# Top-k attention and a tanh-shrink feed-forward on one core: probabilities turned by TensorE in 40 of 144 steps, weight words staged in six places, 128-token feed-forward units, and a look-ahead rate for dealing them

## The chip, the cores and the metric

The program runs on one core of one Trainium2 chip. The metric is the device time of one execution in microseconds (us). The time before is 1709.63 us, the median of three runs (1709.08 to 1714.47).

## What is computed

```python
scores = scale * np.matmul(q, k.transpose(0, 1, 3, 2))     # 8 x 8 heads, 576 x 576, head size 64
kth = np.partition(scores, -top_k, axis=-1)[..., -top_k:-top_k + 1]    # top_k = 32
scores = np.where(scores >= kth, scores, -1000000000.0)
attn = np.exp(scores - np.max(scores, axis=-1, keepdims=True))
attn = attn / (np.sum(attn, axis=-1, keepdims=True) + 1e-09)
x = np.matmul(attn, v)          # then as 4608 tokens x 512
h = x @ w_in                    # 512 x 2048
out = (h - np.tanh(h)) @ w_out  # 2048 x 512
```

The weights arrive as float64, the rest as float32, and all matmuls run in float32, each as two passes in the trace.

## The kernel before

The attention is cut into 144 **steps** (`plan`). A step is 128 query rows of two heads of one batch entry `b`; the last 64 rows of the 576 are gathered over two head pairs into a remainder step (`rem`). For each b there are 16 plain steps, taken in pairs, and 2 remainder steps. Steps are numbered from 0 here. The first `run` takes all of them; the second, exact one is entered only if a flag asks for it.

A step runs through a software pipeline, written out by hand in the loop at the end of `run`. In iteration n the kernel issues, in this order: `values` of step n-4, `spread` of n-3, `mask` of n-1, `search` of n, `spread_keys` of n-2, then `scores` of n+1 and `expo` of n-1, with feed-forward work dealt in between. `manual_schedule` keeps that order on every engine.

- `scores` (L210): TensorE makes the 128 x 576 scores of two heads in PSUM. There is one such buffer, and it comes free when VectorE has done L241 of the step before. ScalarE copies the scores to SBUF (L218).
- `search` (L240 to L251): VectorE folds the two halves of each row by minimum and maximum, then four rounds of MAX8 and MATCH_REPLACE find the 32nd value. A search begins with L240, so L240 marks the start of a step on VectorE.
- `mask` and `expo` (L267 to L317): ScalarE and GpSimd set what is not kept to a very low number and take exponentials; z is the result.
- `turn_z` (L360): VectorE transposes z in blocks of 32 x 32; `spread_keys` (L374): 16 DMAs on SyncE's queue move the blocks, so that `et` holds the transposed z of a pair of steps. There is one `et`.
- `values` (L393, L401): TensorE multiplies `et` with v, once per pair, and turns the spread reciprocals of the sums; ScalarE copies both (L405), and GpSimd multiplies them into the unit's `xT` (L417, L410).

The feed-forward takes **units** of 256 tokens: 16 for the pairs of query blocks and 2 for the remainders of four batch entries each. A unit is 32 items in a first-in-first-out list `work`: 16 of `ffn_h` (L442, four 128 x 256 matmuls, then tanh, copy and subtraction for two of them) and 2 x 8 of `ffn_o` (L462, two 128 x 512 matmuls; the last of a block copies and stores it). `deal` takes items out at four places of an iteration, at a rate that `run` sets anew each time:

```python
more = min([m + 4 for m in done if m + 4 > n], default=n)
share[0] = len(work) / max(more - n, 1)
```

So what is in the list is spread over the iterations until the next unit is ready. At the end of b = 3 and of b = 7, two units come ready one or two steps apart.

The float64 weights are turned into float32 in 32 pieces of 128 x 512 (`convert`): two DMAs of 0.5 MB load the words and the words shifted by three bytes, VectorE does L139, L143 and, later, L149, ScalarE L140, L141 and L146, GpSimd L152. The words lie in two places of `spare`; both DMAs are issued on ScalarE's queue, and a piece's load waits for L149 of the piece two before. The table `many` gives steps 0 to 8 one piece, step 9 four, steps 10 to 16 three each until 32 are done. From step `EARLY` = 17 on, `spare` serves as a second `zx`.

## Time and profile before

| | |
|---|---|
| profiled execution | 1712.53 us, of which the span is 1710.7 us |
| TensorE busy | 1444.8 us (84%) |
| VectorE busy | 1384.2 us (81%) |
| GpSimd busy | 942.8 us (55%) |
| ScalarE busy | 857.9 us (50%) |
| mean granted TensorE clock | 0.94 of full speed |
| moved by DMA | 157.96 MB, mean 92 GB/s |

Busy shares are means over stages with different limits; a stage is read by what its engines do in it, and by what a waiting engine waits for. TensorE's matmuls are pipelined, so a busy TensorE is judged by the spacing of its matmuls. The rows that follow the change come from views of one profiled execution.

### The profile page before, as it was taken

How to read it: one execution, taken by the hardware profiler on the slowest of the kernel's cores; microseconds unless marked ns; L12 is line 12 of the kernel's file. 1: busy time of each engine (PE TensorE's matmuls, PEld its weight loads, DVE VectorE, ACT ScalarE, POOL GpSimd, SP SyncE). 2: the span in 40 equal slices, each digit the busy share in tenths (PEclk: the TensorE clock that was granted, in tenths of full speed). 3: DMA queues.
4: the chain of work that ended last, by engine and by line, in shares of the span. 5: the costliest groups of instructions: out<-in, count | busy, mean ns of one | idle time of the engine just before them, and what ended most of it. 6: DMA issues, size and time to landing. Idle time of an engine off the chain costs nothing.

```text
span 1710.7 us, 24180 instructions
## 1 busy us (share of the span) xinstructions
PE 1444.8 (84%) x6802; PEld 886.7 (52%) x6802; DVE 1384.2 (81%) x3842; ACT 857.9 (50%) x1509; POOL 942.8 (55%) x1517
## 2 busy tenths in 40 slices
PE   1232444899998999899999999899899999899998
PEld 1111332474746474647476564657465646465664
DVE  5986665999989999999945999999999999962800
ACT  2444544455645574556434564566455655442621
POOL 2444544565746584667534665566556666552720
PEclk9956767999999999999999999999999999999999
DMA  6545454453245324532414324533343334310220
GB/s 156 133 136 172 155 175 137 96 109 85 65 102 108 85 66 101 108 82 67 103 28 91 81 62 92 110 86 73 86 105 89 79 84 104 83 48 25 63 49 15
DMA packets 266510, 157.96 MB, mean 92 GB/s; under 512 B 212608, under 2 KB 220800, under 8 KB 266368
## 3 DMA queue, kind: packets, MB, share of 16 engines
q1 hardware_dynamic: 257152, 122.79, 31.9%
q10 hardware_dynamic: 9216, 33.54, 5.8%
q8 instruction: 57, 0.93, 0.2%
q14 instruction: 85, 0.70, 0.1%
HBM read 61.85 MB, written 9.44 MB: 42 GB/s over the span
## 4 chain that ended last, share of the span: by engine, by line
PE 53%; DVE 15%; SPq 14%; DMA 7%; issue 4%; ACT 4%; POOL 2%; ACTq 1%; DVEq 0%; POOLq 0%
PE hps L442 20%; PE ops L462 19%; SPq L374 12%; PE av L393 7%; PE scps L210 6%; DVE m L248 3%; DVE ab L251 3%; DMA spare<-in_moe_w_out_dram 2%; SPq L172 2%; DMA spare<-in_moe_w_in_dram 2%; DVE zx L360 1%; DMA kin<-in_k_dram 1%; DVE f L149 1%; DVE ab L240 1%; DVE ab L243 1%
## 5 line engine op out<-in xcount | busy, mean ns | idle before, releaser
L442 PE MATMUL hps<-xT,w_in 128*128 128x256 f32 x2048 | 484.2, 392 | 56.2 <-ACT g L455 38.4
L462 PE MATMUL ops<-w_out,g 128*128 128x512 f32 x1152 | 526.2, 606 | 0.0
L248 DVE MAX8 m<-ab 128x8 f32<-128x288 f32 (+1 forms) x1152 | 465.0, 446 | 0.0
L442 PEld LDWEIGHTS hps<-xT,w_in 128*128 128x128 f32 x2048 | 390.7, 195 | 137.7 <-ACT g L455 41.5
L283 POOL TENSOR_TENSOR z<-sc,z 128x576 f32<-128x576 f32 x288 | 404.4, 1426 | 59.7 <-ACT z L280 59.7
L251 DVE MATCH_REPLACE8 ab<-m,ab 128x288 f32<-128x288 f32 x864 | 376.7, 445 | 0.0
L462 PEld LDWEIGHTS ops<-w_out,g 128*128 128x128 f32 x1152 | 214.7, 193 | 256.8 <-issue 249.5
L280 ACT ACTIVATE z<-sc,tb 128x576 f32<-128x576 f32 x288 | 207.6, 768 | 200.5 <-POOL tb L267 200.5
L210 PE MATMUL scps<-kT,qT 64*128 64x288 f32 (+1 forms) x1280 | 191.2, 450 | 137.5 <-DVE ab L241 123.1
L456 POOL TENSOR_TENSOR g<-g,th 128x512 f32<-128x512 f32 x144 | 183.6, 1276 | 107.1 <-ACT g L455 103.6
L218 ACT COPY sc<-scps 128x1152 f32<-128x1152 f32 x144 | 160.7, 1116 | 161.7 <-PE scps L210 103.1
L303 ACT ACTIVATE z<-z,nb 128x576 f32<-128x576 f32 x288 | 221.8, 774 | 17.4 <-POOL z L283 17.0
L240 DVE TENSOR_TENSOR ab<-scps,sc 128x576 f32<-128x576 f32 x144 | 106.8, 742 | 151.7 <-ACT sc L218 84.7
L210 PEld LDWEIGHTS scps<-kT,qT 64*128 64x128 f32 (+1 forms) x1280 | 103.8, 186 | 230.9 <-ACT z L303 100.2
L393 PE MATMUL av<-et,vb 128*64 128x256 f32 (+1 forms) x1536 | 157.6, 351 | 65.1 <-DMA et<-zx 41.7
L393 PEld LDWEIGHTS av<-et,vb 128*64 128x64 f32 x1536 | 93.9, 145 | 143.7 <-issue 100.5
L417 POOL TENSOR_TENSOR xT<-xs 128x256 f32<-128x256 f32 x64 | 48.3, 754 | 185.7 <-ACT xs L405 180.8
L405 ACT COPY xs<-av 128x512 f32<-128x512 f32 (+1 forms) x80 | 43.4, 543 | 212.4 <-PE av L401 212.4
L454 ACT ACTIVATE th<-hps 128x512 f32<-128x512 f32 x144 | 84.6, 588 | 93.3 <-PE hps L442 73.0
L243 DVE MAX8 ab<-ab 128x8 f32<-128x288 f32 x288 | 116.6, 447 | 0.0
L360 DVE STREAM_TRANSPOSE zx<-z 128x1152 f32<-128x1152 f32 x80 | 108.7, 1359 | 0.0
L241 DVE TENSOR_TENSOR ab<-scps,sc 128x576 f32<-128x576 f32 x144 | 107.6, 747 | 0.0
(48 smaller groups left out, 1073.9 us busy)
## 6 DMA issues: line engine op xcount, KB each, us to landing
et<-zx SPq DMA_DIRECT2D x576, 72.0 KB, 2.0
et<-spare SPq DMA_DIRECT2D x448, 72.0 KB, 2.0
kin<-in_k_dram SPq DMA_DIRECT2D x128, 72.0 KB, 2.4
qin<-in_q_dram SPq DMA_DIRECT2D x128, 72.0 KB, 2.4
spare<-in_moe_w_in_dram ACTq DMA_DIRECT2D x16, 512.0 KB, 4.1
vb<-in_v_dram SPq DMA_DIRECT2D x64, 128.0 KB, 2.4
spare<-in_moe_w_out_dram ACTq DMA_DIRECT2D x16, 512.0 KB, 3.9
out_dram<-ot SPq DMA_DIRECT2D x32, 256.0 KB, 2.2
```

The source lines that it names most:

```text
L210: nc.tensor.matmul(ps[rows, t, s, 0:S2], qT[g.b, g.hp + i][half(t), qs], kT[g.b, g.hp + i][half(t), ks], start=True, stop=True,)
L218: nc.scalar.copy(sc[:], ps[:, :, :, 0:S2])
L248: nc.vector.max(m[:, t, m8], last[t] if i == rounds - 1 else cur[t])
L251: nc.vector.match_replace(nxt[t], m[:, t, m8], cur[t], NEG)
L280: nc.scalar.activation(zv[:, t, :], scf[:, t, :], AF.Relu, bias=tb[:, t : t + 1], scale=-BIG)
L283: nc.gpsimd.tensor_tensor(zv[:, t, :], scf[:, t, :], zv[:, t, :], ALU.subtract)
L303: nc.scalar.activation(x["zv"][:, t, :], x["zv"][:, t, :], AF.Exp, bias=x["nb"][:, t : t + 1], scale=scale, accum_out=den[:, t : t + 1],)
L374: nc.sync.dma_start(et[group(c), a * w : (a + 1) * w], zx[group(a), c * w : (c + 1) * w])
L393: nc.tensor.matmul(av[half(t), 0, cols], vb[g.b, hp][:, t, c, :] if c < J else vr[g.b, hp][:, t, :], es[:, :, (J + 1) * t + c if c < J els ...
L442: nc.tensor.matmul(ps[:, f % 2, :], w_in[j][:, c, fo : fo + P], u.xT[:, c, :], start=(c == 0), stop=(c == CD - 1),)
L456: nc.gpsimd.tensor_tensor(g, g, th[:], ALU.subtract)
L462: nc.tensor.matmul(cur[u][:], u.g[f // FJ][:, f % FJ, i * P : (i + 1) * P], w_out[f // FJ][:, f % FJ, :], start=(f == 0), stop=(f == CF - 1),)
```

## The change

**Turning.** A step now carries a mark `pe`. It is set in all steps of b = 0, in the last eight plain steps of b = 7 and in all 16 remainder steps: 40 of 144. For these, `turn_pe` replaces `turn_z` and `spread_keys`: TensorE transposes z in nine 128 x 128 pieces into PSUM (L404), and ScalarE copies them to `et` in three copies (L407). Eight of the transposes stand at the start of an iteration, one behind the next scores, and `values` follows in the same iteration. Remainder steps use a place of their own, `et_rem`. The other 104 steps are turned as before.

**Units.** The first two and the last two query blocks are units of 128 tokens, and there are four remainder units of 128 tokens in place of two of 256. `ffn_h` of a small unit takes two 128-wide slices per item, so that an item keeps its size; a small unit has 16 items.

**Rate.** `rate` looks at all units still to come: it takes the lowest rate at which the list does not run dry before any of them, raised where a unit's buffer has to be free earlier.

**Weight words.** There are six places for the words: two in `spare`, and one in each `w_out` tile as long as it is not yet written. The DMAs go on SyncE's queue. k and q of b = 0 are all loaded at the start, those of its last three pairs into room of `w_in[2]` and `w_in[3]`. `many` gives steps 0 and 1 two pieces, 2 to 9 three, 10 four. For later b, k and q are loaded separately and earlier.

```diff
+    def __init__(self, b, hp, qt, unit, col, i=0, nq=1, pe=False):
+        self.b, self.hp, self.qt, self.unit, self.col = b, hp, qt, unit, col
+        self.i, self.nq, self.pe = i, nq, pe
         self.rem = qt == J
+        self.last = i == nq - 1
+
+        self.lag = 2 if pe else 4
...
+    slots = [(spare[:, i], spare[:, 2 + i], 8 * CD) for i in range(2)]
+    for j in reversed(range(WJ)):
+        halves = [
+            flat(w_out[j][:, 2 * i : 2 * i + 2, :]).bitcast(U32).rearrange("p (n w) -> p n w", w=2)
+            for i in range(2)
+        ]
+        slots.append((*halves, (WJ + j) * CD))
...
-        raw = spare[:, i % 2]
-        nc.scalar.dma_start(raw.rearrange("p n w -> p (n w)"), src.bitcast(U32))
-        shifted = spare[:, 2 + i % 2]
-        nc.scalar.dma_start(
-            shifted.rearrange("p n w -> p (n w)").bitcast(U8)[:, 0 : 8 * NW - 4],
-            src.bitcast(U8)[:, 3 : 8 * NW - 1],
+        raw, shifted, _ = slot
+        nc.sync.dma_start(flat(raw), src.bitcast(U32))
+        nc.sync.dma_start(
+            flat(shifted).bitcast(U8)[:, 0 : 8 * NW - 4], src.bitcast(U8)[:, 3 : 8 * NW - 1]
...
+    early = [flat(w_in[j][:])[:, i * S : (i + 1) * S] for j in (2, 3) for i in range(3)]
+
+    def load_rows(name, b, hp, exact):
+
+        if b == 0 and hp and not exact:
+            x = early[2 * hp - 2 + (name == "q")]
+        else:
+            x = ldpool.tile([P, S], FP32, tag=f"{name}in", name=f"{name}in")[:]
+        raw[name, b, hp] = x
...
+    def turn_pe(n):
+
+        g, z = steps[n], st.pop(n)["z"]
+        if g.rem:
+            et = et_rem
+        elif g.i:
+            et = ets.pop(n - 1)
+        else:
+            et = etpool.tile([P, 4 * S], FP32, tag="et", name="et")[:]
+        ets[n] = et
+        et = tiles(et, g.nq)[:, :, :, g.i, :].rearrange("p a k j -> p k a j")
+        for k0 in range(0, KC, J):
+            kn = min(J, KC - k0)
+            zt = zt_ps.tile([P, 512], FP32, tag="zt", name="zt")
+            for k in range(kn):
+                nc.tensor.transpose(
+                    zt[:, k * P : (k + 1) * P], z[:, (k0 + k) * P : (k0 + k + 1) * P], ident[:]
+                )
+            nc.scalar.copy(
+                et[:, k0 : k0 + kn],
+                zt[:, 0 : kn * P].rearrange("p (k a j) -> p k a j", a=NG, j=G),
+            )
+            if k0:
+                yield
...
+    def ffn_h(u, item):
+
+        w = u.n
+        per = 2 * P // w
+        for f in range(item * per, (item + 1) * per):
+            j, fo = f // FJ, (f % FJ) * P
+            s = f * w % 512
+            if s == 0:
+                cur[u] = h_ps.tile([P, 512], FP32, tag="h", name="hps")
+            for c in range(CD):
+                nc.tensor.matmul(
+                    cur[u][:, s : s + w],
+                    w_in[j][:, c, fo : fo + P],
+                    u.xT[:, c, 0:w],
+                    start=(c == 0),
+                    stop=(c == CD - 1),
+                )
+        if item % 2:
+            th = thpool.tile([P, 512], FP32, tag="th", name="th")
+            if item % 4 == 1:
+                u.g.append(gpool.tile([P, 2, 512], FP32, tag="g", name="g"))
...
+            parts = [(0, 1), (2, 3)]
+            if b == 0:
+                parts[0:1] = [(0,), (1,)]
+            if b == B - 1:
+                parts[1:2] = [(2,), (3,)]
+            for a, qts in enumerate(parts):
+                unit = Unit([block(b, qt) for qt in qts], "xT")
+                pe = b == 0 or len(qts) == 1
...
+                    if hp % 2 and a == (0 if b == B - 1 else len(parts) - 1):
+                        steps.append(Step(b, hp - 1, J, rest, b % 2 * R, pe=True))
...
+        for g, after in zip(steps, steps[1:]):
+            if after.pe and not after.rem and not g.pe:
+                g.lag = 3
+
+
+    many = {0: 2, 1: 2, 10: 4} | {n: 3 for n in range(2, 10)}
...
+                if b == 0 and not exact:
+                    m = -4
+                at(m, lambda x=(name, b, hp, exact): load_rows(*x))
+                if x and i < NHP and not exact:
+                    at(-4, lambda: load_piece())
...
+        def load_piece():
+            k = len(loaded)
+            usable = [x for x in free if x[2] > k]
+            if k < pieces and usable:
+                free.remove(usable[0])
+                piece = convert(k, usable[0])
+                next(piece)
+                loaded.append((piece, usable[0]))
...
+        for _ in slots[NHP:]:
+            at(-4, load_piece)
...
+        def rate():
+
+
+            have, low, high = len(work), 0.0, None
+            coming = sorted((t, u.n // 8) for u, t in ready.items() if t > n)
+            for t, k in coming + [(NS + 4, 0)]:
+                r = have / max(t - n, 1)
+                high = r if high is None else min(high, r)
+                have += k
+            for u, t in begun.items():
+                if t > n and u in before:
+                    need = [i + 1 for i, x in enumerate(work) if x[1] is before[u]]
+                    if need:
+                        low = max(low, need[-1] / (t - n))
+            return max(low, high)
...
-            more = min([m + 4 for m in done if m + 4 > n], default=n)
-            if here(-4):
-                values(n - 4)
-            share[0] = len(work) / max(more - n, 1)
...
+            share = rate()
+            if pe:
+                w = turn_pe(n - 2)
+                next(w)
...
+            if pe and steps[n - 2].last:
+                values(n - 2)
...
```

**The words' DMAs, on ScalarE and SyncE, in the first steps.** ScalarE before, the part of step 3 (f and w_in belong to a piece, sc is the copy of the next scores):

```order
L303 ACTIVATE z,den<-z,nb 128x576 x2
L280 ACTIVATE z<-sc,tb 128x576 x2
L140 ACTIVATE f<-f,e_117 128x512
L141 ACTIVATE f<-f,e_119 128x512
L146 ACTIVATE w_in_107<-w_in_107 128x512
L127 DMA spare<-in_moe_w_in_dram 128x1024
L129 DMA spare<-in_moe_w_in_dram 128x4092
L218 COPY sc<-scps 128x1152
```

SyncE of the change, from its first DMA on:

```order
L196 DMA kin<-in_k_dram 32x18x32 x4
L196 DMA qin<-in_q_dram 32x18x32 x4
L146 DMA spare<-in_moe_w_in_dram 128x1024
L147 DMA spare<-in_moe_w_in_dram 128x4092
L196 DMA w_in_109<-in_k_dram 32x18x32 x4
L196 DMA w_in_109<-in_q_dram 32x18x32 x4
L146 DMA spare<-in_moe_w_in_dram 128x1024
L147 DMA spare<-in_moe_w_in_dram 128x4092
L196 DMA w_in_109<-in_k_dram 32x18x32 x4
L196 DMA w_in_110<-in_q_dram 32x18x32 x4
L146 DMA w_out_114<-in_moe_w_in_dram 128x1024
L147 DMA w_out_114<-in_moe_w_in_dram 128x4092
```

Before, the copy of the scores stands behind two DMAs that wait for L149 of the same step; in the change no DMA is left on ScalarE, and the words stand behind k and q on SyncE.

**VectorE in step 5.** Before, from the piece's first operation on:

```order
L139 TENSOR_SCALAR f<-spare 128x512
L143 TENSOR_SCALAR w_in_108<-spare 128x512
L324 RECIPROCAL rd<-rd 128x4
L360 STREAM_TRANSPOSE zx<-z 128x9x4x32
L248 MAX m<-ab 128x8 x2
L251 MATCH_REPLACE ab<-m,ab 128x288 x2
L248 MAX m<-ab 128x8 x2
L251 MATCH_REPLACE ab<-m,ab 128x288 x2
L248 MAX m<-ab 128x8 x2
L149 SCALAR_TENSOR_TENSOR f<-spare,f 128x512
```

In the change, the same place of step 3:

```order
L156 TENSOR_SCALAR f<-spare 128x512
L160 TENSOR_SCALAR w_in_108<-spare 128x512
L156 TENSOR_SCALAR f<-w_out_114 128x512
L160 TENSOR_SCALAR w_in_109<-w_out_114 128x512
L341 RECIPROCAL rd<-rd 128x2
L271 MAX m<-ab 128x8 x2
L274 MATCH_REPLACE ab<-m,ab 128x288 x2
L166 SCALAR_TENSOR_TENSOR f<-spare,f 128x512
L156 TENSOR_SCALAR f<-w_out_113 128x512
L160 TENSOR_SCALAR w_in_109<-w_out_113 128x512
L271 MAX m<-ab 128x8 x2
L274 MATCH_REPLACE ab<-m,ab 128x288 x2
```

Three pieces stand in the step in place of one, and the transposition of z is gone from it.

**TensorE behind the scores of step 74**, where two units have just come ready. Before:

```order
L210 MATMUL scps<-kT,qT 128x288 x4
L462 MATMUL ops<-w_out_114,g 128x512 x4
L393 MATMUL av<-et,vb 64x256 x8
L393 MATMUL av<-et,vr_124 64x256 x2
L401 MATMUL av<-ident,rx 128x4x32 x2
L442 MATMUL hps<-xT,w_in_107 128x256 x16
L442 MATMUL hps<-xT,w_in_108 128x256 x16
L442 MATMUL hps<-xT,w_in_109 128x256 x16
L442 MATMUL hps<-xT,w_in_110 128x256 x4
L210 MATMUL scps<-kT,qT 128x288 x4
```

In the change, behind the scores of step 51 (a remainder step is turned in it):

```order
L233 MATMUL scps<-kT,qT 128x288 x4
L404 MATMUL zt<-ident,z 128x128
L481 MATMUL hps<-xT,w_in_107 128x256 x4
L428 MATMUL av<-spare,vb 64x64 x8
L428 MATMUL av<-spare,vr_121 64x64 x2
L428 MATMUL av<-spare,vb 64x64 x8
L428 MATMUL av<-spare,vr_122 64x64 x2
L436 MATMUL av<-ident,rx 128x128
L481 MATMUL hps<-xT,w_in_107 128x256 x4
L428 MATMUL av<-et,vb 64x256 x8
L428 MATMUL av<-et,vr_122 64x256 x2
L436 MATMUL av<-ident,rx 128x4x32 x2
```

Before, 15 items stand between two groups of scores; in the change each iteration from step 36 to step 137 holds four items (16 of these matmuls, or 8 with w_out), and the last transposition of a turned step stands one item ahead of its values.

## Rows read from the trace of the kernel before

**Rows 1.** The page's slices: busy tenths in 40 equal parts of the span.

```profile
PE   1232444899998999899999999899899999899998
...
DVE  5986665999989999999945999999999999962800
```

**Rows 2.** Busy time by stretch: from:to, its length, each engine, granted clock, DMA share, GB/s.

```profile
17.90:131.00 113.10, 33.55 (x138) 18.50 (x138) 102.66 (x258) 51.19 (x83) 51.24 (x77) 0.80 0.52 134
131.00:310.80 179.80, 76.54 (x343) 49.11 (x343) 116.98 (x277) 88.39 (x150) 86.98 (x105) 0.70 0.47 153
...
380.40:459.70 79.30, 78.98 (x365) 47.91 (x365) 79.30 (x231) 48.28 (x87) 54.72 (x90) 1.00 0.34 82
854.70:918.80 64.10, 63.91 (x269) 42.27 (x268) 19.19 (x55) 17.91 (x33) 20.69 (x28) 1.00 0.19 45
...
1516.00:1582.00 66.00, 65.82 (x286) 43.55 (x282) 17.76 (x52) 18.64 (x33) 20.09 (x27) 1.00 0.10 29
...
1621.50:1710.70 89.20, 81.92 (x288) 48.37 (x286) 3.36 (x5) 15.28 (x28) 16.86 (x21) 0.98 0.14 35
```

**Rows 3.** One line's instructions: L240 in two stretches, first and last start.

```profile
L240 DVE TENSOR_TENSOR ab<-scps,sc x9: 757/758/759, 17.9 to 117.8; 128x576 f32<-128x576 f32 x9
...
L240 DVE TENSOR_TENSOR ab<-scps,sc x10: 736/748/758, 380.4 to 459.7; 128x576 f32<-128x576 f32 x10
```

**Rows 4.** Timeline of the first 158 us: start, length, instruction [idle before it, releaser].

```profile
11.63 0.78 DVE L194 STREAM_TRANSPOSE kT<-kin 128x576 f32<-128x576 f32 x1 [11.63 <-DMA qin<-in_q_dram]
...
14.41 2.29 PE L210 MATMUL scps<-kT,qT 64*128 64x288 f32 x8 [14.41 <-DVE qT L194]
...
149.77 0.43 DVE L139 TENSOR_SCALAR f<-spare 128x512 uint32<-128x512 uint32 x1 [2.92 <-DMA spare<-in_moe_w_in_dram]
...
156.58 1.12 ACT L218 COPY sc<-scps 128x1152 f32<-128x1152 f32 x1 [2.79 <-DVE f L149]
```

**Rows 5.** VectorE's groups by line and form: count | busy us, mean ns | idle before.

```profile
L360 DVE STREAM_TRANSPOSE zx<-z 128x1152 f32<-128x1152 f32 x80 | 108.7, 1359 | 0.0
...
L149 DVE SCALAR_TENSOR_TENSOR f<-spare,f 128x512 uint32<-128x512 uint32 x32 | 28.9, 904 | 5.9 <-ACT f L141 5.8
...
L139 DVE TENSOR_SCALAR f<-spare 128x512 uint32<-128x512 uint32 x32 | 19.9, 623 | 28.4 <-DMA spare<-in_moe_w_out_dram 20.2 <-DMA spare<-in_moe_w_in_dram 8.2
L143 DVE TENSOR_SCALAR w_in<-spare 128x512 uint32<-128x512 uint32 x16 | 13.9, 871 | 5.0 <-DMA spare<-in_moe_w_in_dram 5.0
...
L143 DVE TENSOR_SCALAR w_out<-spare 128x512 uint32<-128x512 uint32 x16 | 9.4, 588 | 6.0 <-DMA spare<-in_moe_w_out_dram 6.0
```

**Rows 6.** TensorE's timeline: one group of scores, and the last unit.

```profile
132.58 1.37 PE L210 MATMUL scps<-kT,qT 64*128 64x288 f32 x8 [1.88 <-DVE ab L241]
...
1645.19 1.95 PE L393 MATMUL av<-et,vb 128*64 128x256 f32 x16
...
1647.51 0.44 PE L401 MATMUL av<-ident,rx 128*128 128x128 f32 x2
1647.78 1.46 PE L442 MATMUL hps<-xT,w_in 128*128 128x256 f32 x6
1649.48 26.60 PE L442 MATMUL hps<-xT,w_in 128*128 128x256 f32 x122 [0.24 <-POOL xT L417]
1675.91 27.63 PE L462 MATMUL ops<-w_out,g 128*128 128x512 f32 x64
```

**Rows 7.** TensorE's timeline at the values of one remainder step (64-wide matmuls).

```profile
692.12 0.69 PE L393 MATMUL av<-et,vb 128*64 128x64 f32 x16
...
695.09 0.69 PE L393 MATMUL av<-et,vb 128*64 128x64 f32 x16 [2.17 <-DMA et<-spare]
...
695.82 0.33 PE L401 MATMUL av<-ident,rx 128*128 128x128 f32 x1
695.99 0.38 PE L442 MATMUL hps<-xT,w_in 128*128 128x256 f32 x1
```

**Rows 8.** TensorE's weight loads of L442, by line and form.

```profile
L442 PEld LDWEIGHTS hps<-xT,w_in 128*128 128x128 f32 x2048 | 390.7, 195 | 137.7 <-ACT g L455 41.5 <-POOL xT L417 24.2 <-issue 18.8
```

More of the change, by code (lines that the diff above doesn't have):

```diff
@@ L476, in ffn @@
     def ffn(u):
-        for f in range(CF):
-            yield CD * (f // FJ + 1), lambda f=f: ffn_h(u, f)
-        for i in range(2):
+        nh = CF * u.n // (2 * P)
+        for item in range(nh):
+            f = (item + 1) * CF // nh - 1
+            yield CD * (f // FJ + 1), u, lambda item=item: ffn_h(u, item)
+        for i in range(len(u.blocks)):
             for part in range(CF // 2):
-                yield CD * (WJ + part // 2 + 1), lambda i=i, part=part: ffn_o(u, i, part)
-    units, rests, steps, first, done, work = {}, [], [], [], {}, []
+                yield CD * (WJ + part // 2 + 1), None, lambda i=i, part=part: ffn_o(u, i, part)
@@ L544, in run @@
[L544 to L552 removed]
+            for x, name in enumerate("kq"):
+                m = max(n - 5 + x, turned.get(name, -4))
+                if b == 0 and not exact:
[3 more added lines that the diff above has]
+                    at(-4, lambda: load_piece())
+                turn = lambda x=(name, b, hp): turn_rows(*x)
+                if 0 < i < NHP:
+                    at_round.setdefault((n - 1, 0), []).append(turn)
+                    turned[name] = n - 1
+                else:
+                    at(n - 3 + x, turn)
+                    turned[name] = n - 3 + x
@@ L557, in between @@
         def between(i):
-            for part, k in parts.pop((n, i), []):
-                next(pieces[k])
-                if part == 2:
-                    converted[0] = k + 1
-                    if k + 2 < len(pieces):
-                        next(pieces[k + 2])
-            if here(-2) and i == 0:
-                invert(n - 2)
-            if here(-2) and i == turn_at(n - 2):
-                turn_z(n - 2)
-        credit, share = 0.0, [0.0]
+            for fn in at_round.pop((n, i), []):
+                fn()
+            if i == 0 and here(-2):
+                invert(n - 2)
+                if not steps[n - 2].pe:
+                    turn_z(n - 2)
+        ready, begun = {}, {}
+        for m, g in enumerate(steps):
+            if g.last:
+                begun.setdefault(g.unit, m + g.lag)
+                if m in done:
+                    ready[g.unit] = m + g.lag + g.pe
+        before, last = {}, {}
+        for u in begun:
+            k = 2 if u.tag == "xT" else 1
+            seen = last.setdefault(u.tag, [])
+            if len(seen) >= k:
+                before[u] = seen[-k]
+            seen.append(u)
+        def rate():
[11 more added lines that the diff above has]
+            return max(low, high)
+        credit = 0.0
         def deal(part):
             nonlocal credit
-            credit += part * share[0]
+            credit += part * share
             while work and credit > 0 and work[0][0] <= converted[0]:
-                work.pop(0)[1]()
+                work.pop(0)[2]()
                 credit -= 1
@@ L591, in run @@
             elif here(-2):
-                invert(n - 2)
-                turn_z(n - 2)
-            if here(-2) and last_of_pair(n - 2):
+                between(0)
+            if here(-2) and not pe and steps[n - 2].last:
                 spread_keys(n - 2)
+            if pe:
+                spread(n - 2)
             deal(0.4)
```

220 lines of the change are left out of this document (94 added, 126 removed).

## The prediction

> **What bounds the kernel now.** I read the slices first: TensorE is nearly idle for the first fifth of the span, both engines are full in the middle, and VectorE is empty at the end [rows 1]. The stretches, cut where a search begins, show four regimes [rows 2].
>
> From 17.9 to 131.0 us run steps 0 to 8 [rows 2, 3], 12.6 us each; VectorE is busy 102.66 of 113.10 us. From 131.0 to 310.8 run steps 9 to 16, 22.5 us each: VectorE is busy only 116.98 of 179.80. Here the words of the weights are late: L139 waits 2.92 us for its DMA, and the copy of the scores stands on ScalarE behind DMAs that wait for L149 [rows 4]. TensorE is busy 110 us up to 310.8, and at a low granted clock (0.80, then 0.70): it has little to do until weights are there.
>
> From step 17 on both engines are nearly full. The nine searches that begin from 380.4 on take 79.30 us, 8.81 each, VectorE without a gap and TensorE busy for 78.98 [rows 2, 3]. Where two units come ready at once, TensorE alone is full: 63.91 of 64.10 us, then 65.82 of 66.00, while VectorE is busy for 19.19 and 17.76. The last 89.2 us hold TensorE's work alone [rows 2]. So behind the head TensorE's total decides, and VectorE is close behind.
>
> **TensorE's total.** Prices, at the full clock: a 128 x 256 pass takes 26.60/122 = 0.218 us, an output pass 27.63/64 = 0.432, a group of scores 1.37, the values of a pair 1647.78 - 1645.19 = 2.59 [rows 6]. The values of a remainder step are two groups, 0.8 and 695.99 - 695.09 = 0.9, together 1.7 [rows 7]. A unit of 256 tokens is 128 passes and 64 output passes, 27.9 + 27.6 = 55.5 us.
>
> Before: 18 units, 999; 144 scores, 197; 64 pairs, 166; 16 remainders, 27; together 1389 us, of a span of 1710.7.
>
> The small units keep their columns. If a 128-wide pass takes half of a 256-wide one, 0.109, nothing is added. The 64-wide ones, 16 in the 0.52 us from 692.12 to the next group, show no floor near that. Eight pairs become 16 single steps; a single's values lie between the remainder's half (0.9) and a pair's (2.59), near the middle by their width, so I take 1.5: 24 for 8 x 2.59 = 21, +3, bounds -6 and +21. A turned step adds nine transposes of 128 columns: 0.17 for one alone (695.82 to 695.99), 0.109 for each that follows, and a second start behind the scores, 1.25 us, or 50 for the 40. The sum is 1442 us, 53 more than before.
>
> **The head.** VectorE's step without conversion is 8.81 - 1.36 (the turn of z, off VectorE in block 0) = 7.45 us [rows 5]. A piece costs 0.62 + 0.73 + 0.90 = 2.26 us, the means over all 32; the undisturbed L139 is 0.43 [rows 4], so a piece may cost 1.5. The k and q turns are 0.78 each [rows 4], six of them inside steps 0 to 2.
> - Steps 0 and 1, two pieces: 2 x (7.45 + 4.5 + 1.56) = 27.0.
> - Step 2: 7.45 + 6.8 + 1.56 = 15.8. Steps 3 to 9, three pieces: 7 x 14.2 = 99.6. Step 10, four: 16.5.
> - Together 159. The first search stood at 17.9 because k and q shared the DMAs with 2 MB of words; now they go first. I take 12.5; the bounds are 17.9 and 10.
>
> So step 11 begins at 171 us, against 179 before; but then all weights are converted and two units are ready, where before 16 pieces were left. This assumes that the words arrive in time: six places let loads run two steps ahead, and ScalarE no longer waits for them. TensorE's clock is the open point: after 14.41 us of idling the first scores take 2.29 us, against 1.37 later [rows 4, 6]. At the lower of its two levels (1.2 and 2.4 GHz) its 8 us of work in each of steps 6 to 10 would be 16, so up to 10 us may be added.
>
> **Behind the head.** Of TensorE's 1442 us, 57 are done by then (11 scores 15, nine turns 11, eight values 12, 11 feed-forward items 19); 1385 are left. From step 36 to step 137 each iteration holds four items, 7.0 us; with 1.37 of scores, 8 x 2.59/18 of values and 2 x 2.95/18 for the remainders that is 9.8 us per step. VectorE has 16 x 8.81 + 2 x 7.45 + 8 x 0.78 = 162 us per 18 steps, 9.0 each. TensorE is the bound there, by 8%, and VectorE's 104 turns and 45 us of idle time at the double units cost or give nothing. Only in steps 18 to 35, where the rate is lower, VectorE decides: 162 against TensorE's 104 + 25 + 21 + 6 = 156 us, +6, and I take 8 with a wait for a late et.
>
> Losses: in the 24 turned steps outside block 0 the values stand one item (1.7 us) behind the last transposition, whose copy queues behind a 1.12 us copy of scores [rows 4] and perhaps tanh work; 1 us each, 24 us, bounds 0 and 3 us each. Elsewhere 1%, 14 us; the full stretches of rows 2 lose 0.3%, and 5% is the upper bound. The 2.17 us wait for a remainder's et [rows 7] goes with the 16 DMAs that each remainder no longer puts on SyncE's queue.
>
> **Sum.** 171 + 1385 + 8 + 24 + 14 = 1602; 7 us from the last output pass to the end, as before (1675.91 + 27.63 against 1710.7), and 1.8 us outside the span (1712.5 less 1710.7): 1611 us. The profiled execution lies 0.2% above the median; I make no correction. Against the execution of before (1712.5) this is 101 us less. There, behind step 16 (310.8 us), some 1306 us of TensorE's work were left by the same prices, and 94 us were lost. Now the head ends 140 us earlier; 79 us more of TensorE's work are left at that point, 53 of them added; and 40 us less are lost, the end included.
>
> **The rivals.** A, slower: **weight loads are not hidden** under 128-wide passes. A load of L442 takes 195 ns [rows 8]. If passes can follow only as fast as loads, each costs 0.195 instead of 0.109: 8 x 128 passes x 0.086 = 88, and 360 transposes x 0.086 = 31, so 1730 us. It makes the kernel slower from 0.18 us per pass on. Against it, loads lie wholly under 256-wide passes at 0.218, and 64-wide ones follow much closer [rows 6, 7]; for it, no row holds a stream of full-width loads at 128 columns. Chance 0.08. The Trainium skill (TensorE: Matmul & The Clock Gate, "The mechanism" in Part 3) says that a weight load overlaps running matmuls only when its row group differs; by that rule A holds here, and the trace disagrees, since 122 passes with loads of the same rows follow at 0.218 us.
>
> B: **words still late.** A step of three pieces stays at 22.5 us, as in steps 9 to 16, instead of 14.2: eight steps, +66, 1677 us. For it: one SyncE queue now carries k, q, v and words. Against it: the waits were those of two places. Chance 0.12.
>
> C: **no losses.** Undisturbed pieces (32 x 0.75 = 24 us) and none of the 38 us of losses: 1549 us. Chance 0.12.
>
> D: the list runs dry, or a unit's buffer holds TensorE up, so that the rate does not do what it says; the program's order shows four items in every iteration, so 0.06, spread to both sides, mostly 1640 to 1700.
>
> **The numbers.** My forecast of 1611 us has 0.62, with a range of its own of 1580 to 1655. The range that should hold the time 8 times in 10 leaves out A and the far side of C: 1550 to 1690. A measurement of this kernel tells about 0.3% from no change. Faster: 0.62 + 0.12 + 0.12 + 0.03 = 0.89. Slower: A, 0.08. The same: 0.03, from D.
>
> **What would show it.** Step 11 begins near 171 us, steps 3 to 9 take 13 to 15 us, and L156 waits little for DMAs. From step 36 on, searches stand 9.8 us apart with VectorE waiting for the copy of the scores and TensorE without gaps. L481's 128-wide passes are 0.109 us apart. I am wrong if the middle stays at 8.8 to 9.5 us per step, if TensorE has idle time there, or if the head is still over 200 us.

## The result, and the profile after

The changed kernel takes 1573.75 us, the median of four runs (1573.65 to 1574.88); the kernel before, beside it, 1710.97 us (1709.08 to 1714.47). The ratio is 0.9197, 95% interval 0.9180 to 0.9214: 137 us less, where 101 were forecast. The profiled execution is one of 1573.68 us with a span of 1571.8.

The slices of the changed kernel, to be laid beside [rows 1]:

```profile
PE   2566699899999999999999999999999999999998
...
DVE  7987689999999999998999999998999899874300
...
PEclk9877799999999999999999999999999999999999
```

TensorE is full from the sixth slice on; before it was from the eighth. The third to fifth slices are still a gap, at a low granted clock.

Busy time by stretch, cut where searches begin (L263, L240 of before): steps 0 to 10, 11 to 17, 18 to 35, 36 to 125, 126 to 137, 138 to 142, and the rest; columns as in [rows 2]:

```profile
11.80:180.80 169.00, 88.78 (x485) 64.89 (x485) 142.51 (x374) 117.41 (x207) 105.44 (x130) 0.80 0.63 209
180.80:240.80 60.00, 57.18 (x405) 39.40 (x406) 55.11 (x176) 44.62 (x87) 40.74 (x71) 0.97 0.16 30
240.80:403.30 162.50, 154.47 (x809) 97.48 (x807) 160.12 (x467) 99.14 (x180) 108.13 (x182) 1.00 0.35 77
403.30:1276.20 872.90, 872.90 (x4532) 550.48 (x4530) 810.56 (x2332) 512.83 (x915) 556.44 (x920) 1.00 0.37 82
1276.20:1391.90 115.70, 115.70 (x582) 66.87 (x579) 105.89 (x312) 65.52 (x118) 70.81 (x123) 1.00 0.35 79
1391.90:1480.10 88.20, 87.88 (x545) 64.02 (x544) 38.29 (x126) 42.48 (x84) 41.05 (x64) 1.00 0.02 7
1480.10:1571.80 91.70, 84.73 (x479) 56.33 (x477) 8.60 (x29) 23.35 (x50) 21.51 (x32) 0.99 0.04 13
```

From step 36 to 137 TensorE has no gap at all: 872.90 of 872.90 us, then 115.70 of 115.70. The 90 steps take 9.70 us each, and VectorE is busy for 93% of them. In steps 18 to 35 it is the other way round: VectorE 160.12 of 162.50, TensorE 154.47. Before, TensorE and VectorE were full in turns [rows 2]; the long stretches at double units, VectorE idle for 45 us each, are gone, and only steps 138 to 142 look like them.

The head ends at 180.8 us with all weights converted; before, at 179, 16 pieces were left. VectorE's timeline in step 10, from its search to that of step 11 (its longest waits, and the two searches):

```profile
153.78 0.75 DVE L263 TENSOR_TENSOR ab<-scps,sc 128x576 f32<-128x576 f32 x1
...
164.20 1.35 DVE L166 SCALAR_TENSOR_TENSOR f<-spare,f 128x512 uint32<-128x512 uint32 x1 [4.28 <-ACT f L158]
170.44 0.43 DVE L156 TENSOR_SCALAR f<-spare 128x512 uint32<-128x512 uint32 x1 [3.30 <-DMA spare<-in_moe_w_out_dram]
...
176.78 0.43 DVE L156 TENSOR_SCALAR f<-spare 128x512 uint32<-128x512 uint32 x1 [2.55 <-DMA spare<-in_moe_w_out_dram]
...
180.84 0.74 DVE L263 TENSOR_TENSOR ab<-scps,sc 128x576 f32<-128x576 f32 x1
```

The waits of L156 answer to that of L139 in [rows 4]. All four pieces lie in `spare`: by step 10 the other four places are `w_out` tiles in use, so the kernel is back at two places, and L156 waits for words again.

Over the whole head VectorE is busy for 142.51 of 169.00 us. The rest is waiting, more for ScalarE's part of a conversion than for words (waited for: us in total, times, longest):

```profile
DVE f L166 <- ACT f L158: 17.3, 8, 4.4
DVE f L156 <- DMA spare<-in_moe_w_out_dram: 6.0, 3, 3.3
```

L160 waits another 2.9 us for words.

The end, on TensorE: values of the last single step, then the last small unit; beside [rows 6]:

```profile
1529.96 1.09 PE L428 MATMUL av<-et,vb 128*64 128x128 f32 x16
...
1531.37 5.32 PE L502 MATMUL ops<-w_out,g 128*128 128x512 f32 x12
1536.53 14.45 PE L481 MATMUL hps<-xT,w_in 128*128 128x128 f32 x128
1550.82 13.90 PE L502 MATMUL ops<-w_out,g 128*128 128x512 f32 x32
1564.64 0.19 PE L730 MATMUL cnt<-ones,anybad 128*1 128x1 f32 x2
```

A 128-wide pass takes (1550.82 - 1536.53)/128 = 0.112 us, an output pass (1564.64 - 1550.82)/32 = 0.432, a single's values 1531.37 - 1529.96 = 1.41. The costliest weight load and the chain on the page of the changed kernel:

```profile
PE 81%; DVE 8%; ACT 4%; SPq 3%; POOL 2%; DMA 1%; issue 1%; DVEq 0%; ACTq 0%; POOLq 0%
...
L481 PEld LDWEIGHTS hps<-xT,w_in 128*128 128x128 f32 x2304 | 399.2, 195 | 63.5 <-issue 14.4
```

TensorE is 81% of the chain that ended last. A load's record is still 195 ns long [rows 8], and passes follow at 112 ns. The records of the loads overlap one another: from 1536.5 to 1550.8 us there are 127 of them, 190 to 192 ns each, in 14.26 us, one every 0.112 us. So the length of a record is not what a load costs.

### The profile page after: what moved, and what is told of

Same layout as the page of the kernel before. It is cut to its first block, busy times and chain, and to the rows that moved or that the text cites. A ratio compares the mean times of both kernels' runs of the same rounds, so it can differ in the third digit from the quotient of the medians.

```text
span 1571.8 us, 25605 instructions
## 1 busy us (share of the span) xinstructions
PE 1463.9 (93%) x7834; PEld 940.6 (60%) x7834; DVE 1322.7 (84%) x3810; ACT 907.7 (58%) x1637; POOL 945.5 (60%) x1533
## 4 chain that ended last, share of the span: by engine, by line
PE 81%; DVE 8%; ACT 4%; SPq 3%; POOL 2%; DMA 1%; issue 1%; DVEq 0%; ACTq 0%; POOLq 0%
PE hps L481 29%; PE ops L502 29%; PE av L428 9%; PE scps L233 9%; PE zt L404 2%; DVE m L271 2%; DVE ab L274 2%; PE av L436 2%; SPq L196 1%; SPq L385 1%; DVE f L166 1%; ACT z L303 1%; DMA spare<-in_moe_w_out_dram 1%; ACT sc L241 1%; ACT f L157 1%
## 5 line engine op out<-in xcount | busy, mean ns | idle before, releaser
L481 PE MATMUL hps<-xT,w_in 128*128 128x256 f32 (+1 forms) x2304 | 476.0, 362 | 0.2 <-POOL xT L452 0.2
L306 POOL TENSOR_TENSOR z<-sc,z 128x576 f32<-128x576 f32 x288 | 400.0, 1411 | 106.3 <-ACT z L303 106.3
L481 PEld LDWEIGHTS hps<-xT,w_in 128*128 128x128 f32 x2304 | 399.2, 195 | 63.5 <-issue 14.4
L502 PEld LDWEIGHTS ops<-w_out,g 128*128 128x128 f32 x1152 | 210.9, 192 | 232.0 <-issue 229.7
L263 DVE TENSOR_TENSOR ab<-scps,sc 128x576 f32<-128x576 f32 x144 | 107.0, 743 | 133.2 <-POOL bad L310 73.3
L233 PE MATMUL scps<-kT,qT 64*128 64x288 f32 (+1 forms) x1280 | 185.5, 439 | 31.0 <-DVE qT L218 28.8
L233 PEld LDWEIGHTS scps<-kT,qT 64*128 64x128 f32 (+1 forms) x1280 | 100.5, 181 | 122.3 <-issue 65.5
L428 PE MATMUL av<-et,vb 128*64 128x256 f32 (+1 forms) x1152 | 133.5, 368 | 39.9 <-ACT et L407 34.2
L452 POOL TENSOR_TENSOR xT<-xs 128x256 f32<-128x256 f32 (+1 forms) x72 | 48.0, 667 | 157.2 <-ACT xs L440 157.0
L428 PEld LDWEIGHTS av<-et,vb 128*64 128x64 f32 x1152 | 77.6, 140 | 100.2 <-ACT et L407 37.8
L336 POOL TENSOR_SCALAR rd<-den 128x2 f32<-128x2 f32 x144 | 33.4, 232 | 146.7 <-ACT z L326 113.1
```

What stands on the lines that cost most here:

```text
L233: nc.tensor.matmul(ps[rows, t, s, 0:S2], qT[g.b, g.hp + i][half(t), qs], kT[g.b, g.hp + i][half(t), ks], start=True, stop=True,)
L306: nc.gpsimd.tensor_tensor(zv[:, t, :], scf[:, t, :], zv[:, t, :], ALU.subtract)
L428: nc.tensor.matmul(av[half(t), 0, cols], vb[g.b, hp][:, t, c, :] if c < J else vr[g.b, hp][:, t, :], es[:, :, (J + 1) * t + c if c < J els ...
L481: nc.tensor.matmul(cur[u][:, s : s + w], w_in[j][:, c, fo : fo + P], u.xT[:, c, 0:w], start=(c == 0), stop=(c == CD - 1),)
L502: nc.tensor.matmul(cur[u][:], u.g[o // 1024][:, o % 1024 // 512, o % 512 : o % 512 + P], w_out[f // FJ][:, f % FJ, :], start=(f == 0), sto ...
```

## The experiments

All twelve start from the changed kernel. "Step n" is the start of its search. The kernel before, run again beside the experiments, took 1706.89 to 1707.76 us, against 1710.97 beside the changed kernel, which was not run again; so differences of a few us are read from the starts of steps in the traces and not from the times.

### Is the middle TensorE's or VectorE's?

**less_vector** shortens one of VectorE's instructions:

```diff
-                nc.vector.max(ab[:, t, S2 : S2 + 8], lo[:, t, :])
+                nc.vector.max(ab[:, t, S2 : S2 + 8], lo[:, t, 0:16])
```

> VectorE does less: the MAX8 L266 looks at 16 of 288 columns, so a part of the smaller halves is left out of the search. It takes 72.7 us busy in the 90 steps from 403.3 to 1276.2 us, 0.81 per step, and some 0.6 of it should go, 86 us over 144 steps. Theory: TensorE's total decides from step 36 on, so only the head (11 steps, 7 us) and steps 18 to 35 (at most 8 us) can gain: 1559 to 1568 us, and the middle stays at 9.70 us per step. Rival: VectorE, whose searches wait only 62 of 872.9 us there, sets the pace together with TensorE: 1530 us or less.

Measured: 1567.39 us (1566.23 to 1567.81), ratio to before 0.9173, 0.9151 to 0.9195. The 90 steps of the middle, and two of VectorE's groups in them:

```profile
395.70:1268.90 873.20, 873.20 (x4537) 550.84 (x4534) 761.83 (x2332) 512.15 (x913) 555.29 (x920) 1.00 0.37 82
```

```profile
L263 DVE TENSOR_TENSOR ab<-scps,sc 128x576 f32<-128x576 f32 x91 | 68.2, 749 | 111.4 <-POOL bad L310 100.2 <-ACT sc L241 11.1
...
L266 DVE MAX8 ab<-ab 128x8 f32<-128x16 f32 x180 | 21.7, 162 | 0.0
```

VectorE does 49 us less (761.83 against 810.56), its idle time before L263 grows by as much (62.3 us in the changed kernel), and the stretch is as long as before: 873.2 against 872.9. What is gained, 6 us, is gained in steps 18 to 35 (156.7 against 162.5), where VectorE was the fuller one; it does 9.7 us less there, and 5.8 of them count before TensorE is full (154.25 of 156.7). The theory holds for both stretches, but not for the head, where it counted on 7 us:

```profile
11.60:179.60 168.00, 89.02 (x485) 65.15 (x485) 137.61 (x374) 117.83 (x207) 107.41 (x130) 0.79 0.62 210
```

VectorE does 4.9 us less in the head, and step 11 comes only 1.2 us earlier. Steps 3 to 6 take 13.4 us as before, and L166's waits for ScalarE's L158 grow from 17.3 to 21.7 us. So VectorE's work alone does not set the head.

**less_tensor** takes work from TensorE:

```diff
-        for f in range(2 * part, 2 * part + 2):
+        for f in range(2 * part, min(2 * part + 2, CF - 1)):
...
-                stop=(f == CF - 1),
+                stop=(f == CF - 2),
```

> TensorE does less: the last of the 16 blocks of hidden units is left out of the output matmuls, 4 passes per unit of 256, 72 passes in all at 0.444 us from start to start: 32 us. Theory: TensorE's total decides from step 36 on: 26 to 32 us less, 1542 to 1548 us, and the middle goes from 9.70 to 9.5 us per step or less. Rival: VectorE, 0.7 us per step behind, or its waits for GpSimd take over at once: a gain under 10 us.

Measured: 1548.72 us (1545.71 to 1549.95), ratio 0.9059, 0.9036 to 0.9083. Steps 18 to 35, and the middle:

```profile
240.90:404.70 163.80, 152.77 (x801) 97.39 (x799) 160.41 (x467) 99.18 (x180) 108.28 (x182) 0.99 0.35 77
404.70:1259.80 855.10, 853.96 (x4486) 542.35 (x4486) 810.28 (x2332) 514.27 (x915) 557.27 (x920) 1.00 0.38 84
```

The middle is 17.8 us shorter, 9.50 per step, where the 44 passes taken out of it are worth 19.5; steps 18 to 35 gain nothing (163.8 against 162.5). The whole gain is 25 of 32 us, 1 us short of the theory's band, and far from the rival. The two runs together show it from both sides: in steps 36 to 125 TensorE's microseconds count, nearly all of them, and VectorE's do not; in steps 18 to 35 VectorE's count, as far as TensorE has room, and TensorE's do not.

### The head, part by part

**two_places** leaves the words their two places of before:

```diff
+    slots = slots[:2]
```

> The change with two places for the words in place of six (still on SyncE's queue). Theory (the places let the words arrive in time): steps 2 to 10 go from 13.4 to 17 us back to about 22 us each, step 11 begins near 240 instead of 181 us, and the whole takes 1615 to 1635 us, since some feed-forward work fills the longer head. Rival (what helped is that ScalarE no longer stands behind the DMAs): step 11 begins before 195 us, total at most 1585 us.

Measured: 1617.08 us (1614.08 to 1618.21), ratio 0.9464, 0.9435 to 0.9493. VectorE's waits up to step 11, which begins at 220.6 us (waited for: us in total, times, longest; lines two higher than in the changed kernel):

```profile
DVE f L158 <- DMA spare<-in_moe_w_out_dram: 24.9, 11, 3.8
DVE f L158 <- DMA spare<-in_moe_w_in_dram: 15.1, 6, 3.5
```

The wait for words is back: 40 us here and 17.9 more at L162, against 8.9 in all in the changed kernel, while the waits for ScalarE's part fall from 17.3 to 6.7. Step 11 and every later step come 40 us later; steps 3 to 6 take 18.3 to 19.3 us instead of 13.4. The theory's time holds, but by two errors: it had put step 11 near 240, and had the feed-forward make up for a part of that, and no later step does.

**scalar_queue** puts the words' DMAs back on ScalarE's queue, with six places:

```diff
-        nc.sync.dma_start(flat(raw), src.bitcast(U32))
-        nc.sync.dma_start(
+        nc.scalar.dma_start(flat(raw), src.bitcast(U32))
+        nc.scalar.dma_start(
```

> The change with the words' DMAs on ScalarE's queue again, six places kept. Theory (places count, not the queue): within 5 us of 1574. Rival (a copy of scores behind waiting DMAs costs 1.4 to 3 us in each of 11 steps): 1590 to 1605 us.

Measured: 1606.94 us (1605.93 to 1608.51), ratio 0.9404, 0.9375 to 0.9433. The theory missed, and the rival is 2 us off. SyncE's first DMAs in the changed kernel (start, length of the issue, operation):

```profile
0.72 2.01 SPq L196 DMA_DIRECT2D kin<-in_k_dram  x4
2.78 2.12 SPq L196 DMA_DIRECT2D qin<-in_q_dram  x4
```

The same in this one:

```profile
0.72 2.38 SPq L196 DMA_DIRECT2D kin<-in_k_dram  x4
5.58 9.36 SPq L196 DMA_DIRECT2D qin<-in_q_dram  x4
```

And VectorE's waits in it up to 60 us:

```profile
DVE kT L218 <- DMA kin<-in_k_dram: 14.7, 1, 14.7
...
DVE qT L218 <- DMA qin<-in_q_dram: 4.1, 1, 4.1
```

With two queues, six pieces' words go out at once, and the k and q that the first search needs land among them: it begins at 23.9 us instead of 11.8. After that each of steps 3 to 6 takes 15.15 us against 13.4, with ScalarE's copy of the scores late (26.6 us of VectorE's waiting in the head, 3.9 in the changed kernel). Step 11 is 31 us late, as is every later step, and the end 33. Of the 31 us the start is 12, which the rival did not have; the other 19 are 1.7 in each of 11 steps, within its 1.4 to 3. The Trainium skill (Trainium Kernel Development and Optimization, "Key Constraints") says that queues of several engines share the same DMA engines, and that issuing from several only saves issue time; the first half agrees with this trace, where in the first 25 us the words' queue takes 72.1% of the 16 engines' time and SyncE's 22.7%, and as for the second, here the second queue cost 12 us at the start alone.

**head_vector** turns block 0's plain steps by VectorE again. Only one `zx` is to be had there, as before, since `spare` holds words:

```diff
-                pe = b == 0 or len(qts) == 1
+                pe = b == B - 1 and a == 1
...
-            last_zx[0] ^= 1
+            last_zx[0] = 0 if n < 18 else 1 - last_zx[0]
```

> The 16 plain steps of block 0 are turned by VectorE and SyncE's DMAs again, as before; all else is as in the changed kernel (1573.75 us). Theory: VectorE sets the head, and a turn costs it the 1.36 us of the kernel before, 16 times: 22 us later by step 18, carried to the end, less at most 8 us because ScalarE no longer stands at copies of transposes while a conversion waits for it (steps 7 to 9 take 15.9 to 17.1 us, steps 3 to 6 13.4): 1588 to 1596 us. Rival 1: those stalls of ScalarE are worth as much as the turns, so nothing changes, within 5 us of 1574. Rival 2: 16 DMAs per pair wait on SyncE's queue for the turn, and the weights' words stand behind them: the head grows by 30 us or more, 1604 us or more.

Measured: 1640.41 us (1639.39 to 1644.93), ratio 0.9617, 0.9582 to 0.9652. Rival 2 holds. VectorE's longest wait between 53 and 234 us, and SyncE's:

```profile
DVE zx L372 <- DMA et<-zx: 62.3, 8, 9.7
```

```profile
SPq L146 <- DVE f L166: 35.1, 13, 7.7
SPq L146 <- DVE f L156: 29.4, 6, 5.4
```

On SyncE's queue the 16 DMAs of a turn stand behind loads of words that wait for a conversion to give back its place (64.5 us of such waits; the changed kernel has 102.5 of them from 51 to 181 us, but no turn's DMAs behind them); the next turn waits for those DMAs, and the next conversion, on VectorE, stands behind the turn. Steps 3 to 9 take 21 to 23 us. Step 18 is 66 us late. So TensorE's transposes seem worth more for the queue that they leave free than for the 22 us of VectorE's time; that split is read from the waits, since no run turns block 0 by VectorE with the DMAs of its turns on another queue than the words.

**pieces_late** spreads the last four pieces:

```diff
-    many = {0: 2, 1: 2, 10: 4} | {n: 3 for n in range(2, 10)}
+    many = {0: 2, 1: 2, 10: 2, 11: 2} | {n: 3 for n in range(2, 10)}
```

> Steps 10 and 11 convert two pieces each, in place of four in step 10. Theory: step 10 took 27.05 us because VectorE waits 9.3 us in it for words that two free places bring too late; two pieces later, loads have a step's time more, so 8 us are gained (1566 us), bounds 0 and 13 us. Rival: what is not waited for in step 10 is waited for in step 11, since both pieces' places come free at the same time as before: within 3 us of 1574.

Measured: 1567.53 us (1567.22 to 1568.45), ratio 0.9184, 0.9154 to 0.9215. Steps 10 and 11 take 13.4 and 11.7 us, 25.1 together against 34.6; step 12 gives 3.9 back (12.4 against 8.5); every step from 18 on begins 6.3 us earlier, and the end too. The theory, within 2 us; but the words' waits in step 10, which it puts at 9.3 us, are 8.3 by the trace (6.0 at L156, 2.3 at L160), and 4.3 more in that step are the wait for ScalarE shown above.

**first_256** makes the first unit one of 256 tokens:

```diff
-                parts[0:1] = [(0,), (1,)]
+                parts[0:1] = [(0, 1)]
```

> The first unit has 256 tokens, in place of two of 128. Theory: TensorE's total decides behind the head, and the 11 feed-forward items that it did before step 11 (about 19 us at the full clock) move behind it: 10 to 19 us later, 1584 to 1593 us, the lower end if the head itself gets shorter without them. Rival: the small first units do nothing, since the list is filled in time either way: within 4 us of 1574.

Measured: 1581.15 us (1579.51 to 1583.04), ratio 0.9264, 0.9232 to 0.9296: 7 us more, between the two. Step 11 comes earlier, at 175.6 us, for steps 7 to 9 take 13.9 to 14.4 us instead of 15.9 to 17.1; but by step 36 it is 6 us late, and stays so. The feed-forward items that the small first unit puts into the head do save TensorE's time later, and they hold up the conversion while they run.

TensorE's timeline of the changed kernel in step 8 shows how they do:

```profile
120.46 0.47 PE L428 MATMUL av<-et,vb 128*64 128x128 f32 x1 [5.69 <-ACT et L407]
...
122.12 3.62 PE L481 MATMUL hps<-xT,w_in 128*128 128x128 f32 x16
125.54 1.31 PE L404 MATMUL zt<-ident,z 128*128 128x128 f32 x8
126.68 1.95 PE L481 MATMUL hps<-xT,w_in 128*128 128x128 f32 x16
128.56 1.24 PE L233 MATMUL scps<-kT,qT 64*128 64x288 f32 x8
129.74 0.33 PE L404 MATMUL zt<-ident,z 128*128 128x128 f32 x1
```

ScalarE's, in the same step:

```profile
126.50 1.07 ACT L407 COPY et<-zt 128x512 f32<-128x512 f32 x2 [3.76 <-PE zt L404]
127.46 1.45 ACT L303 ACTIVATE z<-sc,tb 128x576 f32<-128x576 f32 x2
128.80 0.72 ACT L157 ACTIVATE f<-f,e 128x512 f32<-128x512 uint32 x1
```

And the granted clock (the last but two of a row's columns) around the two items of 16 passes:

```profile
122.10:125.60 3.50, 3.50 (x18) 3.50 (x18) 3.50 (x14) 0.37 (x1) 3.33 (x5) 0.50 0.61 242
126.60:129.80 3.20, 3.20 (x28) 2.60 (x27) 0.43 (x3) 3.17 (x6) 1.47 (x2) 1.00 0.00 0
```

TensorE idles 5.69 us for a copy of its transposes; the item after that runs at 1.2 GHz and takes 3.62 us, the next one at 2.4 GHz 1.95. Behind the slow item stand the transposes, ScalarE waits 3.76 us at L407 for them, and behind L407 stand the conversion's L157 and L158, for which VectorE's L166 waits, 3.28 us. The low clock makes the one item 1.67 us longer; step 8 takes 16.3 us, 2.9 more than each of steps 3 to 6.

### The parts that move work behind the head

**last_256** makes the last unit one of 256 tokens, its steps turned by TensorE in pairs:

```diff
-                parts[1:2] = [(2,), (3,)]
+                parts[1:2] = [(2, 3)]
...
-                pe = b == 0 or len(qts) == 1
+                pe = b == 0 or (b == B - 1 and a == 1)
```

> The last unit has 256 tokens, in place of two of 128; its steps are still turned by TensorE, as pairs. Theory: from step 138 on TensorE had no gap, and its total decides, not what is left behind the last values; the work that moves behind them was done in the 17.6 us steps 138 to 143, which become shorter: within 5 us of 1574. Rival: a unit of 55.5 us behind the last values in place of one of 27.7 ends that much later: 1594 to 1602 us.

Measured: 1572.03 us (1570.94 to 1574.10), ratio 0.9211, 0.9180 to 0.9243. No change, as the theory has it: steps 138 to 142 together are 72.1 us instead of 88.2, what follows 105.6 instead of 91.7:

```profile
1391.90:1464.00 72.10, 71.78 (x452) 52.39 (x451) 38.18 (x123) 38.76 (x76) 36.45 (x56) 1.00 0.03 8
1464.00:1569.60 105.60, 98.58 (x365) 60.60 (x363) 8.40 (x28) 26.44 (x54) 25.00 (x32) 0.99 0.03 11
```

**rem_vector** turns the remainders of b = 1 to 7 by VectorE and DMAs:

```diff
-                        steps.append(Step(b, hp - 1, J, rest, b % 2 * R, pe=True))
+                        steps.append(Step(b, hp - 1, J, rest, b % 2 * R, pe=b == 0))
...
-        et = ets[n] = etpool.tile([P, 4 * S], FP32, tag="et", name="et")
+        if steps[n].rem:
+            et = ets[n] = et_rem
+        else:
+            et = ets[n] = etpool.tile([P, 4 * S], FP32, tag="et", name="et")[:]
```

> The change with the 14 remainder steps of b = 1 to 7 turned by VectorE and 16 DMAs again, into et_rem. Theory (TensorE's total sets the time from step 36 on, VectorE has 0.7 us per step to spare): TensorE loses 14 x 1.25 = 17.5 us of transposes and the waits for ScalarE's copies of them, so 1540 to 1557 us. Rival (VectorE and its waits set the pace): 14 x 1.36 = 19 us more, about 1593 us.

Measured: 1571.47 us (1570.71 to 1574.98), ratio 0.9194, 0.9166 to 0.9221: no change that can be told, so both missed. The middle, and TensorE's values of the last remainders (behind 1391 us):

```profile
405.10:1273.70 868.60, 865.14 (x4449) 543.16 (x4446) 825.12 (x2342) 501.53 (x883) 555.23 (x920) 1.00 0.40 90
```

```profile
L431 PE MATMUL av<-spare,vb 128*64 128x64 f32 x32 | 1.8, 275 | 2.6 <-DMA spare<-zx 2.6
```

The middle is 4.3 us shorter. The transposes of its ten turned steps took 10.4 us there from start to start; 3.5 came back as idle time of TensorE, which had none, and some 2.6 are spread over the other lines. The last remainder then waits 2.6 us for its DMAs, where no more work covers it, and step 138 takes 21.7 us instead of 17.6. TensorE's transposes of the remainders are paid for by the waits they take away.

**old_rate** deals by the kernel before's rule:

```diff
-            share = rate()
+            more = min([t for t in ready.values() if t > n], default=n)
+            share = len(work) / max(more - n, 1)
```

> The change with the rate of before: what is in the list over the iterations until the next unit is ready. Theory (TensorE is full either way, so the order of its work is worth little): VectorE idles again where two units come ready, total within 10 us of 1574. Rival (the even rate is what pays, since VectorE's stops of 45 us each were lost time): 1610 us or more.

Measured: 1597.94 us (1596.03 to 1599.88), ratio 0.9346, 0.9317 to 0.9376: 24 us more, between the two. The same steps in three stretches, 36 to 53, 90 to 125, 126 to 137:

```profile
409.00:598.70 189.70, 189.40 (x983) 120.14 (x980) 162.41 (x468) 104.28 (x187) 113.88 (x186) 1.00 0.34 76
...
952.90:1310.00 357.10, 353.22 (x1812) 221.05 (x1808) 324.12 (x934) 203.19 (x365) 222.65 (x368) 1.00 0.36 81
1310.00:1416.90 106.90, 101.42 (x572) 61.66 (x569) 105.40 (x312) 65.39 (x119) 70.36 (x123) 1.00 0.37 84
```

Steps in which the list is short come in VectorE's time and leave TensorE idle, 5.5 us in the last of these rows; others are long. From step 36 to the end of the span TensorE is without work for 23 us, against 7 in the changed kernel, and it is 6 us late by step 36 already. Of the 26 us by which the profiled span is longer this leaves some 4: for the same work TensorE's busy time behind step 36 is 4.6 us longer (1165.8 against 1161.2), and why it is stays open.

### Putting parts together

**best_a** joins pieces_late, last_256, and rem_vector for b = 1 to 6 (`pe=b in (0, B - 1)` for remainders); **best_b** also spreads the last pieces further:

```diff
-    many = {0: 2, 1: 2, 10: 2, 11: 2} | {n: 3 for n in range(2, 10)}
+    many = {0: 2, 1: 2, 10: 2, 11: 1, 12: 1} | {n: 3 for n in range(2, 10)}
```

> The changed kernel with two pieces each in steps 10 and 11, the last unit of 256 tokens, and the remainders of b = 1 to 6 turned by VectorE. Alone these gave 1567.53, 1572.03 and (with b = 7 too) 1571.47 us against 1573.75. Theory: the parts add up, since each moves the end unchanged: 6 us from the head, 2 from the last unit, and 5 from the turns (the last remainder, where the 14 lost 4 us at step 138, stays on TensorE): 1559 to 1563 us. Rival: the remainders give nothing, since what TensorE saves it waits for et: 1565 us or more.

> As best_a, but the last four pieces are spread over steps 10 (two), 11 and 12 (one each). Theory: VectorE still waited 1.7 us in step 10 and 1.3 us of L156 were stretched in step 11; with more time for the words 1 to 3 us are gained on best_a. Rival: the last words come when TensorE wants them, so the feed-forward is held up: up to 3 us slower than best_a.

Measured: best_a 1563.30 us (1561.08 to 1563.70), ratio 0.9147, 0.9128 to 0.9166; best_b 1564.10 (1561.46 to 1564.95), ratio 0.9150, 0.9130 to 0.9170. best_a is the fastest kernel of this study, 10 us below the change, and 0.3 us over the theory's band. The two can't be told apart: what best_b gains in step 11 (8.8 us against 11.7) step 12 takes back (15.4 against 12.4).

The parts of the change are no shares of its gain. Taken away one at a time, two_places, scalar_queue, head_vector and old_rate cost 43, 33, 67 and 24 us, 167 in all, more than the 137 that the whole change gives: each was measured with the others in place, and turning by VectorE is as dear as that only with the words on SyncE's queue. The early loads of k and q were not taken away by themselves.

## Why the prediction was right, and by how much it was not

The forecast was 1611 us, the result 1573.75: inside the range of 1550 to 1690, but 37 us below the forecast and below that forecast's own range of 1580 to 1655. Against the profiled execution the sum 171 + 1385 + 46 + 7 = 1609 of span (8, 24 and 14 make the 46) stands against 180.8 + 1372.9 + 11 + 7: the busy times of TensorE behind step 11 add up to 1372.9, in 1391.0 us, and 7 of the 18 us without work are the end, from 1564.64 on.

- **What decides.** That TensorE's total decides behind the head, by 8%, and VectorE only in steps 18 to 35, was right: 9.70 us per step against 9.8, 162.5 us against 162, and both experiments of the middle. One sign was wrong: VectorE's 62.3 us of waits before its searches in the middle are not for the copy of the scores, but 58.0 of them for GpSimd's L310.
- **Losses: the term that failed.** The 8 us for steps 18 to 35 came: TensorE idles 8.0 us in them. "1 us each, 24 us" for turned steps (22 of them, by the change's own count of 40 less the 18 of b = 0) and "1%, 14 us" were 3 us of idle time together. In the middle TensorE has no gap at all: the item between the last transposes and the values covers ScalarE's copy, and a loss of dense stretches shows there as wider spacing, not as idle time (next point). This one term is 35 of the 37 us. The other errors cancel by luck, the head 10 us longer and TensorE's busy time 12 us shorter than forecast. "No losses" was one half of rival C, which I gave 0.12; its other half, a faster head, did not come.
- **TensorE's prices** made the right sum from wrong parts. From the start of one pass to that of the next, summed by line behind step 11 (idle time included), against the forecast:

```
                       measured   forecast
feed-forward  L481, L502  1012.9       980
scores        L233         153.9       182
values        L428, L436   182.4       184
transposes    L404          34.2        39
```

  The scores' 1.37 was the length of a group, with a tail that lies under the next instruction: from 128.56 to 129.74 it is 1.18. The feed-forward's 0.218 and 0.432 were those of long streams, and the items in between others cost 3% more (8 us of the 1012.9 are idle time). A turned step is 1.10 (34.2 for 31), forecast 1.25. That the sums agree, 1383 against 1385, is luck: the scores were priced 28 us too high and the feed-forward 33 too low. Those 33 are the kind of loss that the allowance was for, so the same miss can be read as 28 us for the scores and 13 of allowance too many.
- **The head** was 10 us too short. Up to step 3 it was 4.4 us quicker than forecast, steps 3 to 9 took 102.9 us (99.6), step 10 27.05 (16.5). The forecast of 159 us from the first search to step 11 is VectorE's work alone, without a wait. It is 142.5 us of work (a piece takes 1.93 us, not 2.26) and 26.5 of waiting, so two errors of 16 and 26 us nearly cancel, which is luck again, and VectorE's work alone is not what sets the head, as less_vector shows. Two steps of the reasoning failed:
  - "This assumes that the words arrive in time: six places let loads run two steps ahead": so it is up to step 9, but the places in `w_out` run out, and in step 10 there are two, as pieces_late and two_places show. This is 8.9 us of the waiting.
  - ScalarE's part of a conversion was put at nothing, and VectorE waits 17.3 us for it. "ScalarE no longer waits for them" held for the words, but ScalarE now waits for transposes, 3.8 us in step 8, with the conversion behind. The clock, "up to 10 us" in steps 6 to 10, is one link of that chain; first_256 sizes it at some 6 us in steps 7 to 9, clock and items together.
- **Rival A** fell: a 128-wide pass takes 0.112 us, where it needed 0.18 to be slower. Its 195 ns are the length of a load's record, and the records overlap; a pass of half the columns takes half the time (0.112 against 0.218), so no load shows between passes. The rule of the Trainium skill (TensorE: Matmul & The Clock Gate, "The mechanism" in Part 3) that a load overlaps only when the row group differs, to which the same section adds loads into a background weight buffer, doesn't hold in this trace by its row groups: these loads all use the same 128 rows.
- **Rival B** did not come: steps of three pieces took 13.4 to 17.1 us, not 22.5. The kernel with two places shows what late words cost, 40 us in the starts of its steps.
- **Rival D** fell: the rate does what it says, and is worth 24 us.

## What to carry to other kernels

Price a dense engine from the start of one instruction to that of the next, in the mix that will run; on top of such a price, the losses of the full stretches here were nearly nothing. Where one engine is nearly full, count the other engines' parts too: VectorE, busy for 95% of steps 3 to 6, still did not set their length. When an engine is full from some point on, every part ahead of that point is worth its delay at that point (delays of 40 and of 31 us went unchanged through all later steps here). Moving work about behind it is worth nothing as long as the engine stays full (last_256); an order that lets it run dry costs (old_rate, 24 us). Taking transfers off a queue that loads are waiting in can be worth more than the engine time that goes with them.

## What had not been expected of the hardware

- Weight loads of 128 rows and 128 columns, recorded at 190 to 192 ns each, follow one another every 0.112 us, and so do the 128-wide passes that use them.
- Words issued on a second queue delayed the first k and q: 8.5 and 9.0 us from issue to landing instead of 2.5, and SyncE's issue of four of them took 9.36 us instead of 2.12.
- After an idle time of 5.69 us the granted clock was 0.50, and an item of 16 passes took 3.62 us; 4.6 us later it was 1.00, and the same item took 1.95.
